# Gated linear attention followed by a Mamba output block on one core: alpha copied to SBUF ahead of its scans, idle matmuls and a new order in the first turns

## The chip, the cores and the metric

The kernel runs on one core of a Trainium2 chip. A core has engines that run side by side, each with its own stream of instructions, which it works through in the order in which the program gave them: TensorE (PE) multiplies matrices and transposes through an identity matrix, VectorE (DVE) works element by element and runs the scans, ScalarE (ACT) applies functions and copies, GpSimd (POOL) does slow element work, and SyncE (SP) only issues transfers. The engines wait for each other with semaphores. Matrix results land in PSUM, everything else lives in SBUF, inputs and outputs in device memory.

The metric is the device time of one execution in microseconds (us), as the median of several. All numbers below are of this one core.

## The reference

```python
# attention: batch 4, heads 8, sequence 768, head size 48; alpha between 0.8 and 1.0
for t in range(S):
    state = alpha[:, :, t, :, None] * state + einsum('bhd,bhde', k[:, :, t], v[:, :, t])   # outer product
    y[:, :, t] = einsum('bhd,bhde->bhe', q[:, :, t], state)
x = y.transpose(0, 2, 1, 3).reshape(4, 768, 384)          # heads side by side

# gated SSM: d_model 384, d_inner 512
proj = x @ w_in;  val, gate = proj[..., :512], proj[..., 512:]
for t in range(S):
    h = exp(A_log) * h + val[:, t];  ys[:, t] = h
out = (silu(gate) * ys) @ w_out
```

The weights and inputs of the second block come as 64-bit floats and are turned into 32-bit ones in the kernel.

## The kernel before

The sequence of each of the 4 batches is cut into 3 groups of 256 steps, which gives 12 turns, `n = 0 .. 11`. A turn has a *front* (products of the decays by scans: V from the end backwards, P from the start forwards, then K and Q scaled by them, then the scores `sc` within a block, masked into A), a *back* (block states S_n, values, result `x_sb`, and its transposition into `xT`) and the *ssm* of an earlier turn (`pj`: projection by `w_in`, scan `hh`, gate `sg`, product `f`, and `o`: projection by `w_out`). Each is a generator; a string of letters says in which order the generators are stepped, and so in which order every engine gets its instructions. F is a step of this turn's front, A of the next turn's front, B of the back, P and H of the last turn's ssm, O of the ssm two turns ago, U converts one weight unit to 32 bits (12 units), C checks the range of V, G and M start loads of later turns, L issues transfers that are waiting, E computes exp(A_log).

```python
    def front(n):
        ...
            aT = p1.tile([C, NP, GC], FP32, name="aT")
            ...
            for jj, js in enumerate(halves):                       # two halves
                tp = aT[:, js] if by_vector else turned("a", jj)   # by_vector: n >= 4. Else: TensorE transposes into PSUM
                for u in range(2):
                    nc.vector.tensor_tensor_scan(out=V[:, 2 * jj + u, GC - 1::-1], data0=tp[:, u, ::-1], ...)
                if not by_vector:
                    nc.scalar.activation(aT[:, js], tp, AF.Copy)
                yield
            K = ...                    # tp of k (TensorE), times V (VectorE)        yield
            keys_back(K, s["Kn"], ps_tp)   # tpk: TensorE; Kn: ScalarE copies       yield
            ...                        # iV0 = 1/V, P: two scans over aT, per half   yield, yield
            Q = ...                    # tp of q (TensorE), times P (VectorE)        yield
            ...                        # sc: TensorE; A: copy_predicated (VectorE)   yield

    def back(n):
        ...
            first, last = n % NG == 0, n % NG == NG - 1      # NG = 3
            S_n = p2.tile([C, GR, NP, D], FP32, name="S_n")
            if not first:
                vg = nc.vector if n < 2 else nc.gpsimd
                vg.tensor_mul(S_n[:, 0], S_end[0], s["V"][:, :, 0:1].to_broadcast([C, NP, D]))
            zv = block_states(s["Kn"], v_sb, ps_y, "y")      # z on TensorE
            ...                                              # S_n, S_end: VectorE adds   yield
            yv = values_inside(A, v_sb, ps_y, p2, 1)         # y on TensorE, then "fence" on ScalarE   yield
            values_before(yv, s["Q"], S_n, first, 1)         # y on TensorE; ScalarE copies y to x_sb  yield
            features(x_sb, xs[n], ps_tp)                     # tpx on TensorE, xT on ScalarE           yield

    def convert_unit(u):               # 2 instructions on ScalarE, 2 on VectorE, 1 on GpSimd
        ...

    def load_batch(b):                 # called by M in turns 2, 3 and 5
        t = big.tile(..., name="batch")
        ...                            # 6 memsets on GpSimd, then transfers put on the waiting list

        both = (nc.sync, nc.scalar)    # the first transfers
        load(0, "a", both, 2)
        load(0, "kq", both)
        nc.scalar.dma_start(out=a_log, ...)
        load(0, "v"); fetch_units(0, 2); load(1, "a"); fetch_units(2, 4); load(1, "k")
        fetch_units(4, 6); load(1, "q"); fetch_units(6, 8); load(1, "v")

        early = ["FFFFEFFFGBFUUAABUBCAB", "UFFUFPUFGHPBFUCUHPBAAHBPHBUU",
                 "FPHPFFUFHPUHMLFBLPLFALOLHBLABLALOLBC", "OLFFPLFFMHPLHFBLAAPLHBLACLPBHLOLB",
                 "FLFFFCLPHPLHFBMPBLAHPLBHALOBLO"]
        usual = "FLPFFFFHLPBFHWMPLBAHOLABPLHBOLC"
```

Of the kernel before, what the change touches and what calls it, by code (L numbers as in the profile page):

```python
# [18 lines left out]
def kernel(  # L19
# [185 lines left out]
    def step(gen):  # L205
        if gen is not None:
            next(gen, None)


    def ranged(ctx):  # L210
# [122 lines left out]
        def front(n):  # L333

            pad = pads[n % NBUF]
            b, g = divmod(n, NG)
            by_vector = n >= BY_VECTOR
            V = Vs[n % 2]
            s = st[n] = dict(V=V)

            def turned(name, jj):
                tp = ps_tp.tile([C, 2, GC], FP32, tag="tp", name="tp")
                for u in range(2):
                    j = 2 * jj + u
                    for c in range(G):
                        nc.tensor.transpose(tp[:, u, ds(c * C, C)], pad[name][:, c, j], ident)  # L346
                return tp

            def squares(name, dst):
                nc.vector.transpose(dst, batches[b, name][:, :, ds(g * GC, GC)])  # L350

            halves = [slice(2 * jj, 2 * jj + 2) for jj in range(NP // 2)]
            aT = p1.tile([C, NP, GC], FP32, name="aT")
            if by_vector:
                squares("a", aT)
            for jj, js in enumerate(halves):
                tp = aT[:, js] if by_vector else turned("a", jj)
                for u in range(2):
                    nc.vector.tensor_tensor_scan(out=V[:, 2 * jj + u, GC - 1::-1], data0=tp[:, u, ::-1],  # L359
                                                 data1=bias[:, 1:2].to_broadcast([C, GC]), initial=1.0,  # L360
                                                 op0=ALU.mult, op1=ALU.max)
                if not by_vector:
                    nc.scalar.activation(aT[:, js], tp, AF.Copy)
                yield
            K = p1.tile([C, NP, GC], FP32, name="K")
            if by_vector:
                squares("k", K)
            for jj, js in enumerate(halves):
                nc.vector.tensor_mul(K[:, js], K[:, js] if by_vector else turned("k", jj), V[:, js, 1:GC + 1])
            yield  # L370
            s["Kn"] = p1.tile([C, G, NP, C], FP32, name="Kn")
            keys_back(K, s["Kn"], ps_tp)
            yield
            iV0 = p2.tile([C, NP], FP32, name="iV0")
            P = p1.tile([C, NP, GC], FP32, name="P")
            for jj, js in enumerate(halves):
                nc.vector.reciprocal(iV0[:, js], V[:, js, 0])
                for u in range(2):
                    nc.vector.tensor_tensor_scan(out=P[:, 2 * jj + u, :], data0=aT[:, 2 * jj + u, :],  # L379
                                                 data1=bias[:, 1:2].to_broadcast([C, GC]),  # L380
                                                 initial=iV0[:, 2 * jj + u:2 * jj + u + 1],
                                                 op0=ALU.mult, op1=ALU.max)
                yield
            Q = s["Q"] = p2.tile([C, NP, GC], FP32, name="Q")
            if by_vector:
                squares("q", Q)
            for jj, js in enumerate(halves):
                nc.vector.tensor_mul(Q[:, js], Q[:, js] if by_vector else turned("q", jj), P[:, js])
            yield
            sc = ps_sc.tile([C, 2, 512], FP32, tag="sc", name="sc")  # L390
            scv = sc.rearrange("p i (x t) -> p i x t", t=R)
            for c in range(G):
                for j in range(NP):
                    for r in range(NR):
                        for i in range(2):
                            rows, steps = ds(DP * i, DP), ds(c * C + R * r, R)
                            nc.tensor.matmul(scv[ds(R * r, R), i, c * NP + j, :], K[rows, j, steps],
                                             Q[rows, j, steps], start=True, stop=True, skip_group_check=True)
            for i in range(2):
                nc.vector.copy_predicated(out=A[:, i].rearrange("p x t -> p (x t)"),  # L400
                                          mask=mask[:, ds(i * GP * R, GP * R)], data=sc[:, i])
            yield
# [9 lines left out]
        def back(n):  # L412

            s = st.pop(n)
            v_sb = vs.pop(n)
            first, last = n % NG == 0, n % NG == NG - 1
            S_n = p2.tile([C, GR, NP, D], FP32, name="S_n")
            if not first:
                vg = nc.vector if n < 2 else nc.gpsimd
                vg.tensor_mul(S_n[:, 0], S_end[0], s["V"][:, :, 0:1].to_broadcast([C, NP, D]))  # L420
            zv = block_states(s["Kn"], v_sb, ps_y, "y")
            S_end[0] = None if last else p2.tile([C, NP, D], FP32, name="S_end")
            for x in range(GR):
                src = zv[:, x % NR, x // NR]
                dst = S_n[:, x + 1] if x + 1 < GR else S_end[0]
                if first and x == 0:
                    nc.scalar.activation(dst, src, AF.Copy)
                elif dst is not None:
                    nc.vector.tensor_add(dst, S_n[:, x], src)  # L429
            yield  # L430
            yv = values_inside(A, v_sb, ps_y, p2, 1)
            yield
            values_before(yv, s["Q"], S_n, first, 1)
            x_sb = p1.tile([C, G, DM], FP32, name="x_sb")
            xv = x_sb.rearrange("p g (i f) -> p i g f", i=2)
            ys = yv.rearrange("p i g j e -> p i g (j e)")
            nc.scalar.activation(xv[:, 0], ys[:, 0], AF.Copy)
            for r in range(NR):
                nc.scalar.activation(xv[ds(R * r, R), 1], ys[ds(R * (1 - r), R), 1], AF.Copy)
            yield  # L440
            xs[n] = p2.tile([C, NK, GC], FP32, name="xT")
            features(x_sb, xs[n], ps_tp)
            yield
# [10 lines left out]
        for name in "aqk":  # L454
            clear_pads(1, name)
        nc.vector.memset(A, 0.0)
        both = (nc.sync, nc.scalar)
        load(0, "a", both, 2)
        load(0, "kq", both)
        nc.scalar.dma_start(out=a_log, in_=moe_A_log.rearrange("(a p) -> p a", p=C))  # L460
        load(0, "v")
        fetch_units(0, 2)
        load(1, "a")
        fetch_units(2, 4)
        load(1, "k")
        fetch_units(4, 6)
        load(1, "q")
        fetch_units(6, 8)
        load(1, "v")
        to_convert = iter(range(len(units)))  # L470

        def any_outside():
# [19 lines left out]

        early = ["FFFFEFFFGBFUUAABUBCAB", "UFFUFPUFGHPBFUCUHPBAAHBPHBUU",
                 "FPHPFFUFHPUHMLFBLPLFALOLHBLABLALOLBC", "OLFFPLFFMHPLHFBLAAPLHBLACLPBHLOLB",
                 "FLFFFCLPHPLHFBMPBLAHPLBHALOBLO"]
        usual = "FLPFFFFHLPBFHWMPLBAHOLABPLHBOLC"
        ending = ["PHRPHOPHRPHO", "OO"]
        fronts = {n: front(n) for n in range(N)}  # L500
        backs = {n: back(n) for n in range(N)}
        ssms = {}
        final = any_outside()

        def load_group(n):
            load(n + 2)
# [14 lines left out]
        with tc.manual_schedule():  # L521
            for n in range(N + 2):
                for word in early[n] if n < len(early) else usual if n < N else ending[n - N]:
# [4 lines left out]
                    elif word == "B":  # L528
                        step(backs[n])
                    elif word in "PH":  # L530
                        if n - 1 not in ssms:
                            ssms[n - 1] = ssm(n - 1, xs.pop(n - 1), prev_h, p2, ps_mm)
                        step(ssms[n - 1])
                    elif word == "O":
                        step(ssms[n - 2])
                    elif word == "C":
                        check_products(n)
                    elif word == "U":
                        convert_unit(next(to_convert))
                    elif word == "R":  # L540
                        step(final)
                    elif word == "E":
                        nc.scalar.activation(a_dec, a_log, AF.Exp)
                    elif word == "W" and n - NG - 3 in parts:
                        check_part(n - NG - 3)
                    elif word == "G":
                        load_group(n)
                    elif word == "L":
                        issue(4096 if n < NG else 3072)
                    elif word == "M":  # L550
                        make_ready(n)
# [192 lines left out]
```

## Time and profile before

| what | value |
|---|---|
| device time, median of 3 | 315.44 us (315.3 to 320.01) |
| span of the profiled execution | 312.9 us |
| ScalarE busy | 130.6 us (42%), 279 instructions |
| GpSimd busy | 44.6 us (14%), 58 instructions |
| transfers | 33.74 MB, mean 108 GB/s |
| one turn of the TensorE in its even stretch (tpk at 201.04 us to tpk at 222.87 us) | 21.83 us |
| `pj`: 576 matmul records of 128x256 | 134.6 us |
| `o`: 192 matmul records of 128x384 | 66.5 us |

How to read it: the profile lists the instructions of every engine with start and length, and for the idle time before one, which event ended it. In rows of instructions merged in order of time, the columns are start, length (both us), engine, source line, operation, result and operands, count, and in brackets the idle time before it and what ended that. A 32-bit matmul of `pj` or `o` appears as two records, a 32-bit transpose as one. PEclk is the clock that TensorE was granted, 1.00 being full.

### The profile page before, as it was taken

The numbers are of one execution on the slowest core, as the hardware profiler recorded it, in microseconds if no ns is written. First come the engines' busy times: TensorE is split into PE (matmuls) and PEld (weight loads), VectorE is DVE, ScalarE is ACT, GpSimd is POOL, SyncE is SP. The second block draws the span as 40 slices with busy tenths as digits, with TensorE's granted clock in tenths as the row PEclk, the third lists the DMA queues.
The fourth block names the chain that finished last, engine by engine and source line by source line (L and its number), as shares of the span: only waits on it lengthen the run. The fifth ranks groups of instructions, "written<-read, shape, count | busy, mean of one in ns | idle before, by whom it ended". The sixth has DMA issues, their size and how long they took to land. (4 is left out here: it accounts for less than half of the span.)

```text
span 312.9 us, 9330 instructions
## 1 busy us (share of the span) xinstructions
PE 285.9 (91%) x4041; PEld 226.3 (72%) x4041; DVE 218.3 (70%) x383; ACT 130.6 (42%) x279; POOL 44.6 (14%) x58
## 2 busy tenths in 40 slices
PE   3857997993999999999999999999999999999992
PEld 1636876881788788786787787787877877877760
DVE  4695887853728898688598796986986987932320
ACT  1338566420461561411535515625534545355120
POOL 5021410276009100055000000000000000000000
PEclk9995899997799999999999999999999999999998
DMA  8999999126769999996899998503303012000001
GB/s 134 218 259 214 177 271 166 34 40 79 108 86 172 98 116 119 118 183 111 107 112 163 125 131 145 137 2 129 78 2 127 27 57 95 5 28 26 27 31 57
DMA packets 161411, 33.74 MB, mean 108 GB/s; under 512 B 151120, under 2 KB 160336, under 8 KB 161360
## 3 DMA queue, kind: packets, MB, share of 16 engines
q1 hardware_dynamic: 157632, 32.45, 65.8%
q10 hardware_dynamic: 3728, 0.59, 1.4%
q8 instruction: 34, 0.56, 0.9%
q14 instruction: 17, 0.14, 0.2%
HBM read 28.31 MB, written 4.72 MB: 106 GB/s over the span
## 5 line engine op out<-in xcount | busy, mean ns | idle before, releaser
L121 PE MATMUL pj<-xT,w_in 128*128 128x256 f32 x576 | 134.6, 384 | 0.0
L121 PEld LDWEIGHTS pj<-xT,w_in 128*128 128x128 f32 x576 | 107.2, 191 | 16.5
L136 PE MATMUL o<-w_out,f 128*128 128x384 f32 x192 | 66.5, 491 | 0.0
L130 ACT ACTIVATE sg<-pj 128x256 f32<-128x256 f32 x48 | 18.4, 383 | 97.2 <-DVE hh L125 97.1
L136 PEld LDWEIGHTS o<-w_out,f 128*128 128x128 f32 x192 | 34.9, 190 | 20.2
L125 DVE TENSOR_TENSOR_SCAN hh<-a_dec,hh,pj 128x256 f32<-128x256 f32 x32 | 23.6, 737 | 23.0 <-PE pj L121 23.0
L131 DVE TENSOR_TENSOR f<-sg,hh 128x256 f32<-128x256 f32 x48 | 20.4, 426 | 27.4 <-ACT sg L130 27.4
L379 DVE TENSOR_TENSOR_SCAN P<-aT,iV,bias 128x256 f32<-128x256 f32 x48 | 33.9, 749 | 1.2
L257 POOL MEMSET batch<- 32x1536 f32 x18 | 24.7, 1372 | 25.1 <-DMA batch<-in_q_dram 18.4
L346 PE MATMUL tp<-ident,pads 128*128 128x128 f32 x96 | 17.4, 326 | 6.8 <-POOL mask_f L328 3.2
L420 POOL TENSOR_TENSOR S_n<-S_end,V 128x192 f32<-128x192 f32 x7 | 3.6, 514 | 140.3 <-DVE V L359 114.9
L175 PE MATMUL y<-v_sb,A 64*64 64x48 f32 x768 | 15.8, 228 | 7.6 <-DVE A L400 5.3
L175 PEld LDWEIGHTS y<-v_sb,A 64*64 64x64 f32 x768 | 13.8, 141 | 12.2 <-DVE A L400 6.9
L139 ACT ACTIVATE o_sb<-o 128x384 f32<-128x384 f32 x24 | 11.7, 488 | 22.9 <-PE o L136 20.9
L359 DVE TENSOR_TENSOR_SCAN V<-aT,bias 128x256 f32<-128x256 f32 x32 | 20.2, 677 | 0.3
L193 PEld LDWEIGHTS y<-S_n,Q 64*64 64x64 f32 x704 | 13.4, 144 | 9.2 <-ACT fence L180 4.7
L346 PEld LDWEIGHTS tp<-ident,pads 128*128 128x128 f32 x96 | 12.9, 164 | 9.6 <-POOL mask_f L328 3.2
L193 PE MATMUL y<-S_n,Q 64*64 64x48 f32 x704 | 14.9, 230 | 4.0 <-ACT fence L180 4.0
L429 DVE TENSOR_TENSOR S_n<-S_n,z 128x192 f32<-128x192 f32 x32 | 11.3, 352 | 8.6 <-POOL S_n L420 7.5
L149 ACT ACTIVATE Kn<-tpk 128x512 f32<-128x512 f32 x24 | 13.2, 594 | 9.0 <-PE tpk L148 8.2
L400 DVE COPY_PREDICATED A<-mask,sc 128x512 f32<-128x512 uint8 x24 | 16.0, 719 | 0.0
L148 PE MATMUL tpk<-ident,K 128*128 128x128 f32 x96 | 14.6, 300 | 1.5 <-ACT xT L203 1.4
(64 smaller groups left out, 303.6 us busy)
## 6 DMA issues: line engine op xcount, KB each, us to landing
v_sb<-in_v_dram SPq DMA_DIRECT2D x24, 192.0 KB, 4.7
out_dram<-o_sb SPq DMA_DIRECT2D x24, 192.0 KB, 2.6
staging<-in_moe_w_in_dram SPq DMA_DIRECT2D x8, 384.0 KB, 5.0
part<-in_moe_w_in_dram SPq DMA_DIRECT2D x8, 384.0 KB, 5.8
staging<-in_moe_w_out_dram SPq DMA_DIRECT2D x4, 384.0 KB, 6.3
batch<-in_alpha_dram SPq DMA_DIRECT2D x4, 384.0 KB, 8.0
batch<-in_k_dram SPq DMA_DIRECT2D x4, 384.0 KB, 7.5
batch<-in_q_dram SPq DMA_DIRECT2D x4, 384.0 KB, 8.5
```

Source lines behind the costliest of these rows:

```text
L121: nc.tensor.matmul(pj[:, i, :], w_in[:, kk, i, ds(cc * C, C)], xT[:, kk, :], start=(kk == 0), stop=(kk == NK - 1))
L125: nc.vector.tensor_tensor_scan(out=hh, data0=a_dec[:, cc:cc + 1].to_broadcast([C, GC]), data1=pj[:, 0, :], initial=prev_h[cc][:, GC - 1:GC ...
L130: nc.scalar.activation(sg, pj[:, 1, :], AF.Silu)
L131: nc.vector.tensor_mul(f[:, cc, :], sg, hh)
L136: nc.tensor.matmul(o, f[:, cc, ds(c * C, C)], w_out[:, cc, :], start=(cc == 0), stop=(cc == NI - 1))
L175: nc.tensor.matmul(yv[at, i, c, j, :], A[rows, i, c * NP + j, :], v_sb[rows, c, NP * i + j, :], start=(c == 0 and j == 0), stop=False, ski ...
L193: nc.tensor.matmul(yv[at, i, c, j, :], Q[rows, j, ds(R * x, R)], S_n[rows, x, j, :], start=False, stop=(c == G - 1 and j == NP - 1), skip_ ...
L257: nc.gpsimd.memset(tv[ds(DP * i + W, W), :, D - W:W], 1.0 if name == "a" else 0.0)
L346: nc.tensor.transpose(tp[:, u, ds(c * C, C)], pad[name][:, c, j], ident)
L359: nc.vector.tensor_tensor_scan(out=V[:, 2 * jj + u, GC - 1::-1], data0=tp[:, u, ::-1], data1=bias[:, 1:2].to_broadcast([C, GC]), initial=1 ...
L379: nc.vector.tensor_tensor_scan(out=P[:, 2 * jj + u, :], data0=aT[:, 2 * jj + u, :], data1=bias[:, 1:2].to_broadcast([C, GC]), initial=iV0[ ...
L400: nc.vector.copy_predicated(out=A[:, i].rearrange("p x t -> p (x t)"), mask=mask[:, ds(i * GP * R, GP * R)], data=sc[:, i])
```

## The change

The change does five things.

1. In the front, ScalarE copies the transposed alpha from PSUM into `aT` first, and the V scans read `aT`. Before, the scans read PSUM and the copy followed them.
2. In the backs of turns 1 and 2 the first product of S_n goes to VectorE; before, only that of turn 1. From turn 4 on (turn 3 has none) it stays on GpSimd.
3. A one-element-wide activation at the start makes ScalarE load its table of functions early. The k and q of turn 0 are all issued by SyncE, and weight units, k, q and v are fetched in another order.
4. A new letter D runs two matmuls of the identity with itself into an unused PSUM tile. Nothing reads it. There are 13 in turn 0 and one in turn 1.
5. The strings of turns 0 to 4 and the usual one are put in another order.

It is meant to shorten the first turns, in which the engines wait for one another, and to keep TensorE from dropping to a lower clock there.

```diff
             for jj, js in enumerate(halves):
-                tp = aT[:, js] if by_vector else turned("a", jj)
+                if not by_vector:
+                    nc.scalar.activation(aT[:, js], turned("a", jj), AF.Copy)
                 for u in range(2):
-                    nc.vector.tensor_tensor_scan(out=V[:, 2 * jj + u, GC - 1::-1], data0=tp[:, u, ::-1],
+                    nc.vector.tensor_tensor_scan(out=V[:, 2 * jj + u, GC - 1::-1], data0=aT[:, 2 * jj + u, ::-1],
                                                  ...
-                if not by_vector:
-                    nc.scalar.activation(aT[:, js], tp, AF.Copy)
                 yield
 ...
-                vg = nc.vector if n < 2 else nc.gpsimd
+                vg = nc.vector if n < NG else nc.gpsimd
 ...
-        both = (nc.sync, nc.scalar)
-        load(0, "a", both, 2)
-        load(0, "kq", both)
+        load(0, "a", (nc.sync, nc.scalar), 2)
+
+        nc.scalar.activation(bias[:, 0:1], bias[:, 0:1], AF.Copy)
         nc.scalar.dma_start(out=a_log, in_=moe_A_log.rearrange("(a p) -> p a", p=C))
-        load(0, "v")
-        fetch_units(0, 2)
-        load(1, "a")
+        load(0, "k")
+        fetch_units(0, 1)
+        load(0, "qv")
+        fetch_units(1, 2)
+        load(1, "ak")
         fetch_units(2, 4)
-        load(1, "k")
+        load(1, "q")
         fetch_units(4, 6)
-        load(1, "q")
+        load(1, "v")
         fetch_units(6, 8)
-        load(1, "v")
 ...
-        early = ["FFFFEFFFGBFUUAABUBCAB", "UFFUFPUFGHPBFUCUHPBAAHBPHBUU",
-                 "FPHPFFUFHPUHMLFBLPLFALOLHBLABLALOLBC", "OLFFPLFFMHPLHFBLAAPLHBLACLPBHLOLB",
-                 "FLFFFCLPHPLHFBMPBLAHPLBHALOBLO"]
-        usual = "FLPFFFFHLPBFHWMPLBAHOLABPLHBOLC"
+
+        early = ["DDFFDDFFUDDFFFGBUDFEDAADDCBDAUDBDB", "FFUFUFGBUFACPHBUUPHABDUPHPBHUU",
+                 "FPHPFFHUPFFHBOFMLPLCALABLHABLOLBL", "OLFFPLFAAFMLBFHPLBHPLHABLPBHLCOL",
+                 "FLFFFPLBHPLFHCPLBAHALOLBMPHBLO"]
+        usual = "FLPFFFFHLPBFHPLBHAAWMOLBPLHBOLC"
 ...
+        def warm():
+
+            t = ps_mm.tile([C, 2, GC], FP32, tag="mm", name="warm")
+            for i in range(2):
+                nc.tensor.matmul(t[:, i, 0:C], ident, ident, start=True, stop=True)
 ...
+                    elif word == "D":
+                        warm()
```

## The prediction

> **What bounds the kernel now.** I read the page first, busy shares and the 40 slices.
>
> ```profile
> PE 285.9 (91%) x4041; PEld 226.3 (72%) x4041; DVE 218.3 (70%) x383; ACT 130.6 (42%) x279; POOL 44.6 (14%) x58
> ...
> PE   3857997993999999999999999999999999999992
> ...
> POOL 5021410276009100055000000000000000000000
> PEclk9995899997799999999999999999999999999998
> ```
>
> TensorE is full from slice 12 (about 86 us) to the end: that stretch is bound by it. The holes are in the first ten slices, where the granted clock dips twice (slices 4 and 5, slices 10 and 11), each time with or after a hole. The page's chain of waits has a single link, the last copy, so I worked from the windows and from the rows in order of time. The windows (columns: stretch, length, busy us of PE, weight load, DVE, ACT, POOL with counts, granted clock, DMA share, GB/s):
>
> ```profile
> 20.00:24.00 4.00, 0.45 (x15) 0.32 (x15) 3.93 (x8) 1.05 (x2) 1.70 (x2) 0.97 0.96 260
> 24.00:28.00 4.00, 3.74 (x56) 3.35 (x56) 1.18 (x2) 2.88 (x8) 1.01 (x1) 0.50 0.95 221
> ...
> 72.00:76.00 4.00, 0.41 (x2) 0.00 (x0) 0.45 (x2) 0.00 (x0) 3.32 (x4) 0.87 0.61 77
> 76.00:84.00 8.00, 6.51 (x142) 5.52 (x143) 6.29 (x12) 2.96 (x8) 0.00 (x0) 0.64 0.76 108
> 84.00:306.00 222.00, 220.83 (x3059) 173.84 (x3058) 161.14 (x278) 93.06 (x204) 19.55 (x18) 1.00 0.64 92
> ```
>
> Two holes, each followed by half clock; after 84 us only 1.2 us of 222 are idle. Who makes the second hole, from the rows in order of time:
>
> ```profile
> 66.46 8.42 POOL L257 MEMSET batch<- 32x1536 f32 x6
> 74.96 0.51 POOL L420 TENSOR_TENSOR S_n<-S_end,V 128x192 f32<-128x192 f32 x1
> 75.51 1.13 DVE L429 TENSOR_TENSOR S_n<-S_n,z 128x192 f32<-128x192 f32 x3 [7.52 <-POOL S_n L420]
> ...
> 77.33 0.44 PE L175 MATMUL y<-v_sb,A 64*64 64x48 f32 x2 [4.92 <-DVE A L400]
> ...
> 77.93 1.95 PE L175 MATMUL y<-v_sb,A 64*64 64x48 f32 x62 [0.16 <-DVE A L400]
> ```
>
> In turn 2 the first product of S_n stands on GpSimd behind six memsets of `batch`. VectorE waits 7.52 us for it, the masked copy to A comes after it in VectorE's stream, and TensorE stands for A. The first hole:
>
> ```profile
> 7.01 1.28 ACT L363 ACT_TABLE_LOAD   x1 [7.01 <-DMA pads<-in_k_dram]
> ...
> 22.39 0.60 ACT L363 ACTIVATE aT<-tp 128x512 f32<-128x512 f32 x1 [4.20 <-DVE V L359]
> ...
> 24.26 1.95 PE L193 MATMUL y<-S_n,Q 64*64 64x48 f32 x48 [2.63 <-ACT fence L180]
> ...
> 32.54 3.49 PE L121 MATMUL pj<-xT,w_in 128*128 128x256 f32 x12
> ```
>
> ScalarE copies turn 1's alpha only after VectorE's scans, and `fence`, which the next TensorE work needs, stands behind those copies. The first projection starts at 32.54 us, at less than full clock (3.49 us; 2.7 later).
>
> **The sum of what is lost.** At full clock, start to start in the even stretch, a turn costs: tpk 0.87, four projection chunks 10.77, z 0.96, sc 1.06, y inside 1.08, y before 1.08, tpx 0.65, o 5.36, together 21.83 us, as the turn from 201.04 to 222.87 us has it; eight transposes cost 0.97 where pads are turned. I charge each stretch with its work at those prices. Up to 35.87 us: 40 transposes (4.85), two tpk (1.74), z, sc, two y (4.17), tpx (0.65), one chunk (2.69), sum 14.1, so 21.8 us are lost. To 54.60 us: work 15.9 of 18.7, 2.8 lost. From 54.60 to the o that ends near 72.3, nothing. To 82.35: work 2.65 (two y, four transposes) of 10.1, 7.4 lost. Later three small ones (102 to 105, 109 to 110, 143 to 145 us): 1.7. In all some 34 us; a change to the early order has no more to win.
>
> **What the Trainium skill says.** "TensorE: Matmul & The Clock Gate", section "What's actually happening": TensorE runs at half clock after an idle window of about 3.4 us and at full clock after about 3.4 us of work. The trace agrees: 0.45 us busy in 20 to 24, then 0.50; 4.9 us idle at 72.4, then 0.64 over 76 to 84. The same page, "Part 4: PE-mode transpose", says transposes do not count as work in the same way; no row here separates that, but it speaks for D being true matmuls. "ScalarE: Activation LUTs", section "What ACT_TABLE_LOAD costs": about 1283 ns for the load; here 1.28 us. "PSUM — Partial Sum Buffer", section "Engine vs sequencer instructions": ScalarE, VectorE and GpSimd queues are strictly first in, first out; the product at 74.96 right behind the last memset agrees.
>
> **Part by part.**
>
> *Product of turn 2 on VectorE.* One 128x192 product of 0.35 us (as turn 1's at 40.52) in place of a 7.52 us wait. VectorE was idle there, so nothing is pushed. TensorE's hole (4.9 idle plus about 2.1 of half clock in y, transposes and y, with the rest) goes: 7.4 us, of which I count 7.0 to 7.5. The next user of GpSimd's product is turn 4 (turn 3 is first in its batch); the second set of memsets can start once q of turn 3 is turned and takes 8.4 us, which ends before turn 4's back.
>
> *Alpha by ScalarE first.* Costs one 0.6 us copy before the first scan of each half, for turns 0 to 3. In turn 0: transposes of half 0 end near 5.1, copy to 5.9 (the early activation has the table in by about 5.3), scans 5.9 to 7.2, half 1 to 8.5, against 7.81 before. But K can then start on its transposes, which before waited for the table load and both copies (9.00 us): K ends near 10.8 against 11.68. In turn 1 the copies no longer wait for the scans, so `fence` is free of them.
>
> *Reordered conversions.* A unit costs VectorE 1.1 us. One now stands before P and one before the masked copy. By VectorE's stream: K to 10.8, unit to 11.9, P (3.1) to 15.1, Q (1.3) to 16.4 (15.98 before, but one unit further), S_n to 17.5, unit to 18.6, A to 20.0, V of turn 1 to 22.45. ScalarE: copies to 19.0, range check (2.7) to 21.7, fence 21.9, unit to 23.2. TensorE: y inside to 21.1, k of turn 1 to 22.4, y before to 23.7. x_sb to 25.3, xT to 26.9 (31.1 before). This is where TensorE gains, but not all of it: the built order now puts z, sc and half of turn 2's alpha ahead of the first projection. sc waits for Q of turn 1: K to 23.8, unit, P half, unit, P half, unit to 30.3, Q to 31.6. So sc 31.4 to 32.5, four transposes, and the first chunk at 33.0, no earlier than before. From there: chunk, y (A at 36.0), chunk to 39.8, transposes, y before, D, two chunks to 47.2, tpx, k of turn 2, and turn 1's first chunk at about 49.4 against 54.60. Gain 5.2 us.
>
> *Idle matmuls.* 14 D of two 128x128 matmuls; half of a 256-wide one (2.69/6 = 0.45), so 0.45 us each at full clock, 6.3 in all. They lie almost all in gaps (turn 0 has more than 20 us of them); in the walk above they are included. What they buy is that I may use full-clock prices: before, transposes and tpk from 9.0 to 13.1, and everything from 24 to 34, ran at about double length.
>
> *Order in turns 2 to 4 and after.* I followed the built order with the durations above through turn 2: every wait of TensorE (K at 51.8, Q at 60.1, A near 65) ends before its turn in the stream. The third turn's tpk comes near 76.3 against 89.29, 13.0 earlier, which is the sum of the two gains (12.6) and small change. TensorE's order in the usual turn is unchanged.
>
> Sum: 5.2 + 7.4 = 12.6. I take off about 0.5 for new small waits that a walk by hand does not see: 315.4 - 12.1 = 303.3, rounded to 303.
>
> **The rivals.**
>
> *Transfers become the limit.* The first 20 loads run at about 200 GB/s without a pause until 44 us, in both kernels. v of turn 1 is now the 14th load of about 0.39 MB, 5.5 MB, which by the bytes moved before (4.9 MB at 24 us, 5.8 at 28) lands near 27.5, when z wants it; alpha of turn 2 lands near 32.7, wanted at 32.5. So there is no margin, and SyncE issues four more transfers. If this binds, the prologue gains 2 instead of 5: 306. For: those figures. Against: no long wait on a transfer now.
>
> *The clock drops all the same.* By the walk TensorE stands from 29.6 to 31.3 and in several gaps before. If half clock returns about 29 to 36 us, 2 to 3 us come back: 305 to 306.
>
> *The hole moves.* If VectorE, now the bound of the first 36 us, or PSUM buffers stop TensorE in turns 2 to 4, part of the 7.4 returns: 305 to 308. For: three scan blocks in a row before Q of turn 3. Against: VectorE had 11.5 us of work in 54 to 72 and slack of some 5 us per turn.
>
> *Better than the walk.* The 1.7 us of late holes close and the prologue gains 7: 300.
>
> **Range and chances.** 303.0, and 299.5 to 308 for 8 in 10; upward is wider since three of four rivals point there. The turn 2 product alone is worth 2.3%, so the first parts would have to lose for the whole to stay within 2% (309.1): faster 0.93, same 0.05, slower 0.02.
>
> **What would show it.** In the profile after: the wait of S_n on GpSimd at 7.5 us gone and TensorE without a hole between turn 2's o and y; xT of turn 0 near 27; the first chunk still near 33; turn 1's first chunk near 49; tpk of turn 3 near 76; PEclk without the two dips; turns of 21.8 us from there. I am wrong if z waits for v, if half clock shows about 30, or if a turn after the third is longer than 21.9.

## The result and the profile after

The changed kernel takes 305.9 us (median of four executions, 304.69 to 307.32) against 315.64 us (four, 315.3 to 320.01): a ratio of 0.9662, with a 95% interval from 0.9567 to 0.9758. The prediction was 303.0 us, in a range of 299.5 to 308. So the direction and most of the size came out, and about 3 us of the expected gain are missing. The ratios here and below are not quotients of the medians, and they leave out disturbed executions, which medians and ranges hold, so the two can differ a little.

The 40 slices of the page of the changed kernel (TensorE, GpSimd, granted clock):

```profile
PE   7988699999999999999999999999999999999991
...
POOL 5111321283092000190000000000000000000000
PEclk9999999999999999999999999999999999999998
```

The hole in slice 10 is gone, and so are both dips of the clock. What remains is the 6 in slice 5 (30.3 to 37.8 us). Its stretches in the windows (columns as before: length, busy us of PE, weight load, DVE, ACT, POOL, granted clock, DMA share, GB/s):

```profile
24.00:28.00 4.00, 3.07 (x44) 2.38 (x36) 3.90 (x7) 2.56 (x6) 1.01 (x1) 1.00 1.10 269
28.00:32.00 4.00, 2.61 (x74) 1.95 (x72) 3.93 (x8) 3.90 (x8) 1.45 (x2) 1.00 1.04 268
32.00:36.00 4.00, 2.56 (x71) 2.11 (x72) 3.76 (x10) 0.32 (x1) 0.87 (x2) 1.00 0.76 127
72.00:76.00 4.00, 4.00 (x76) 2.67 (x75) 3.52 (x8) 1.73 (x4) 0.00 (x0) 1.00 0.59 74
```

From 72 to 76 us TensorE works all the time (0.41 us of 4 before). From 24 to 36 it has full clock, but is busy for 8.24 of 12 us only. The rows of TensorE there say what it waits for:

```profile
30.99 0.68 PE L160 MATMUL z<-v_sb,Kn 64*64 64x48 f32 x32 [0.81 <-DMA v_sb<-in_v_dram]
32.08 1.53 PE L396 MATMUL sc<-Q,K 64*64 64x64 f32 x64 [0.41 <-DVE Q L387]
34.34 0.30 PE L346 MATMUL tp<-ident,pads 128*128 128x128 f32 x1 [0.73 <-DMA pads<-in_alpha_dram]
35.13 0.52 PE L346 MATMUL tp<-ident,pads 128*128 128x128 f32 x3 [0.49 <-DMA pads<-in_alpha_dram]
35.48 2.76 PE L121 MATMUL pj<-xT,w_in 128*128 128x256 f32 x12
```

Three waits are new: half of z stands for v of turn 1, sc for Q, and the transposes for turn 2's alpha, in two pieces. They hold back the first projection chunk to 35.48 us (33.0 in the walk), although its operand `xT` is ready at 27.4. The third turn in order of time, GpSimd, VectorE and TensorE mixed:

```profile
62.25 8.45 POOL L257 MEMSET batch<- 32x1536 f32 x6
...
66.07 0.35 DVE L419 TENSOR_TENSOR S_n<-S_end,V 128x192 f32<-128x192 f32 x1
66.53 1.13 DVE L428 TENSOR_TENSOR S_n<-S_n,z 128x192 f32<-128x192 f32 x3
...
70.09 1.15 PE L175 MATMUL y<-v_sb,A 64*64 64x48 f32 x64
```

The product is done on VectorE in 0.35 us while the memsets run, and the 64 records of y follow without a wait.

Where the time went, by marks on TensorE in the two profiled executions (spans 312.9 and 302.7 us):

| mark | before | after | gained up to here | predicted |
|---|---|---|---|---|
| first chunk of turn 0 starts | 32.54 | 35.48 | -2.9 | -0.5 |
| first chunk of turn 1 starts | 54.60 | 51.87 | 2.7 | 5.2 |
| tpk of turn 3 starts | 89.29 | 79.19 | 10.1 | 13.0 |
| from there to the end (length) | 223.6 | 223.5 | 10.2 | 12.1 (12.6 less 0.5) |

So 7.4 us came between the second and third mark, and 2.7 of 5.2 before the second. After the third, nothing changes: a turn is still 21.83 us, tpk to tpk (124.78 to 146.61). The profiled execution is the fastest of the four; the median lost about 1 us more.

### The profile page after: what moved, and what is told of

Its sections match the earlier page's. It is cut to its first block, busy times and chain, and to the rows that moved or that the text cites. A ratio compares the mean times of both kernels' runs of the same rounds, so it can differ in the third digit from the quotient of the medians.

```text
span 302.7 us, 9427 instructions
## 1 busy us (share of the span) xinstructions
PE 288.3 (95%) x4097; PEld 229.7 (76%) x4097; DVE 221.0 (73%) x384; ACT 131.5 (43%) x280; POOL 44.4 (15%) x57
## 5 line engine op out<-in xcount | busy, mean ns | idle before, releaser
L378 DVE TENSOR_TENSOR_SCAN P<-aT,iV,bias 128x256 f32<-128x256 f32 x48 | 35.8, 788 | 0.8
L360 DVE TENSOR_TENSOR_SCAN V<-aT,bias 128x256 f32<-128x256 f32 x48 | 29.6, 673 | 5.7 <-ACT aT L358 5.4
L257 POOL MEMSET batch<- 32x1536 f32 x18 | 24.7, 1371 | 23.9 <-PE tp L346 13.1
L346 PE MATMUL tp<-ident,pads 128*128 128x128 f32 x96 | 15.8, 302 | 2.1 <-DMA pads<-in_alpha_dram 1.2
L396 PE MATMUL sc<-Q,K 64*64 64x64 f32 x768 | 14.4, 221 | 1.9 <-DVE Q L387 1.4
L193 PEld LDWEIGHTS y<-S_n,Q 64*64 64x64 f32 x704 | 12.2, 134 | 5.1 <-issue 5.0
L125 DVE TENSOR_TENSOR_SCAN hh<-a_dec,pj 128x256 f32<-128x256 f32 x16 | 10.9, 679 | 7.1 <-PE pj L121 7.1
L346 PEld LDWEIGHTS tp<-ident,pads 128*128 128x128 f32 x96 | 12.0, 153 | 4.8 <-DMA pads<-in_alpha_dram 2.0
L160 PEld LDWEIGHTS z<-v_sb,Kn 64*64 64x64 f32 x768 | 12.4, 134 | 4.3 <-issue 3.3
L175 PEld LDWEIGHTS y<-v_sb,A 64*64 64x64 f32 x768 | 12.5, 134 | 4.0 <-issue 1.9
L396 PEld LDWEIGHTS sc<-Q,K 64*64 64x64 f32 x768 | 12.6, 135 | 3.7 <-DVE Q L387 2.8
```

The costliest lines, as they stand in the source:

```text
L125: nc.vector.tensor_tensor_scan(out=hh, data0=a_dec[:, cc:cc + 1].to_broadcast([C, GC]), data1=pj[:, 0, :], initial=prev_h[cc][:, GC - 1:GC ...
L257: nc.gpsimd.memset(tv[ds(DP * i + W, W), :, D - W:W], 1.0 if name == "a" else 0.0)
```

## The experiments

Three theories were to be told apart. **Alpha late**: the missing time is turn 2's alpha, which lands after the walk's 32.7 us. **VectorE late**: Q of turn 1 is late since VectorE's work takes longer beside GpSimd's additions. **Clock**: half clock in some executions. And each part of the change was to be valued by itself. Kernels of a group share their chip and their executions of the kernel before: 315.31 us in the first group, 315.71 in the second and 315.93 in the third.

### First group: the parts

**The changed kernel again**, with no edit:

> The changed kernel once more, as the yardstick on this chip and for a second trace. Both theories: 304.5 to 307.5 us, ratio to before about 0.968. If the spread of its earlier executions (304.7 to 307.3) comes from TensorE's clock, a slower execution shows a stretch of half clock in the first 40 us that the first trace (mean clock 0.997) does not have.

Measured: 306.36 us (306.1 to 309.03), ratio 0.9733 [0.967, 0.9796]. TensorE's rows in its profiled execution (span 304.2 us):

```profile
35.80 0.87 PE L346 MATMUL tp<-ident,pads 128*128 128x128 f32 x3 [0.86 <-DMA pads<-in_alpha_dram]
36.46 4.00 PE L121 MATMUL pj<-xT,w_in 128*128 128x256 f32 x12
```

Alpha's last piece is 0.7 us later than in the first profile, and the same 12 records of the first chunk take 4.00 instead of 2.76 us; the granted clock is 0.63 from 36 to 40 us. The third turn's tpk starts at 80.83 (79.19). So the rival of the prediction in which the clock drops all the same came true here, after the wait for alpha. The first chunk is 1.2 us longer by it; 0.7 of that is left at turn 1's first chunk, which starts at 53.50.

**The turn 2 product alone**, in the kernel before:

```diff
-                vg = nc.vector if n < 2 else nc.gpsimd
+                vg = nc.vector if n < NG else nc.gpsimd
```

> The kernel before with one line changed: the first product of S_n of turn 2 on VectorE. Theory 1 (the product behind the memsets alone makes the hole of turn 2): 7 to 7.5 us less, about 308, ratio 0.977, TensorE without a hole between turn 2's o and y. Theory 2 (the hole moves, the new order of turns 2 to 4 is needed as well): 2 to 5 us less, and another wait stands before y of turn 2.

Measured: 309.0 us (307.64 to 310.33), 0.9794 [0.9734, 0.9855]. The hole is gone (y follows o directly at 71.62 us), and tpk of turn 3 starts at 81.72, 7.6 us earlier than in the kernel before. 0.7 of that is already there at turn 1's first chunk (53.88 against 54.60), which comes ahead of the edit, so the hole gave 6.9. Of the 7.6, 1.08 us return at 86.44, where transposes wait for ScalarE's copy of Kn of turn 3, and 6.4 us are left of the span. That is a little less than the first theory said. The rest of the change adds some 2.6 us by the medians (309.0 to 306.36); the intervals of the two ratios overlap.

**Without the idle matmuls** (all the rest of the change):

```diff
                     elif word == "D":
-                        warm()
+                        pass
```

> The changed kernel without the 14 pairs of idle matmuls (D does nothing); all else the same. Theory 1 (VectorE's chain and the transfers set the first 36 us, the idle matmuls only keep the clock up): half clock returns somewhere between 12 and 30 us, and 1 to 3 us are lost. Rival (the clock carries most of what the first turns gain): 4 to 6 us slower than the changed kernel. Second rival (they only stand in the way): 0.5 to 1 us faster, because k of turn 0 is transposed earlier.

Measured: 308.24 us (306.51 to 312.2), 0.975 [0.9675, 0.9826], which overlaps with the kernel that has them. Without them the clock is 0.76 from 24 to 28 us and 0.81 from 28 to 32, yet TensorE reaches turn 0's y before at 21.96 instead of 23.33 us and ends sc of turn 1 at 31.7 instead of 33.6. All of that lead is lost in one row:

```profile
34.73 0.30 PE L346 MATMUL tp<-ident,pads 128*128 128x128 f32 x1 [2.98 <-DMA pads<-in_alpha_dram]
```

Alpha comes when it comes, whether TensorE waits 3 us for it or 0.8. After a second wait of 0.59 us the clock is 0.57 from 36 to 40 us, and the first chunk takes 4.44 us. So a lead of TensorE is lost as long as alpha is late; the median is 1.9 us above that of the kernel with the idle matmuls, which fits the first theory, but the overlap leaves it open.

**The turn 2 product back on GpSimd**, in the changed kernel:

```diff
-                vg = nc.vector if n < NG else nc.gpsimd
+                vg = nc.vector if n < 2 else nc.gpsimd
```

> The changed kernel with the product of turn 2 back on GpSimd. The memsets run from 62.25 to 70.7 us in the changed kernel, and y of turn 2 starts at 70.09. Theory 1: the product comes at about 70.8, S_n and A follow to 73.3, y moves to about 72.5 to 73.5, so 2.5 to 4 us slower than the changed kernel, with or without half clock after it. Rival (the product is worth 7.4 us in any order): 7 to 8 us slower.

Measured: 306.48 us (305.61 to 308.18), 0.9699 [0.965, 0.9748]: no slower. Both theories missed. The third turn, mixed engines:

```profile
64.31 0.90 POOL L419 TENSOR_TENSOR S_n<-S_end,V 128x192 f32<-128x192 f32 x1
...
65.27 8.45 POOL L257 MEMSET batch<- 32x1536 f32 x6
...
72.26 1.15 PE L175 MATMUL y<-v_sb,A 64*64 64x48 f32 x64
```

In the new string of turn 2 (`FPHPFFHUPFFHBOFML...`) B stands ahead of M; in the old one (`FPHPFFUFHPUHMLFB...`) M came first. GpSimd so gets the product ahead of its six memsets. From turn 1's first chunk (54.03) to turn 3's tpk (81.36) TensorE takes 27.33 us here, 27.32 in the changed kernel and 34.69 before. So the hole has two cures, either of which is enough: another engine for the product in the old order, or the rest of the change with the old engine. That it is the place of B and M in it is read from these rows; the two letters were not moved by themselves.

### Second group: why the first turns gained less

**The changed kernel**, as the yardstick:

> The changed kernel as the yardstick beside the next three: 305 to 307 us. In the first trace the first projection of turn 0 started at 35.48 us at full clock, in the second at 36.46 at about half clock, both after a wait for alpha of turn 2. Theory: every execution has that wait, and the half clock comes with the longer ones.

Measured: 307.16 us (305.8 to 309.77), 0.9743 [0.9703, 0.9784]. In its profile TensorE waits 1.29 and 0.72 us for the two pieces of alpha, and the first chunk runs from 36.38 at full clock (2.75 us). These waits are the longest of the three profiles of this kernel, so half clock does not go with the longer ones, as the theory had it. Its third turn's tpk is at 80.10.

**Turn 2's alpha fetched ahead of weight units 6 and 7**; nothing else is moved but these two units, which come after it:

```diff
         load(1, "v")
-        fetch_units(6, 8)
 ...
-            load(n + 2)
             if n == 0:
+                load(2, "a")
+                fetch_units(6, 8)
+                load(2, "kqv")
                 fetch_units(8, ...)
+            else:
+                load(n + 2)
```

> The changed kernel with alpha of turn 2 fetched ahead of weight units 6 and 7 instead of behind them; nothing else differs. Theory (the transfer of alpha of turn 2 is what the first projection waits for): alpha lands near 31 to 32, the waits at 34 to 36 us go, the first projection starts near 34.0, at full clock, 1.5 to 3 us faster than the changed kernel. Rival (VectorE's chain up to Q of turn 1 is the bound all the same): the projection starts earlier but VectorE's scans and products behind it do not, and turn 1's first chunk stays at 51.9 or later; 0 to 0.5 us.

Measured: 303.66 us (302.49 to 304.29), 0.9621 [0.9592, 0.9649]: 3.5 us less than the yardstick, and with no overlap of the executions. SyncE's issues for that alpha in the changed kernel:

```profile
28.43 3.23 SPq L110 DMA_DIRECT2D pads<-in_alpha_dram  x4
```

and in this one:

```profile
25.93 4.37 SPq L110 DMA_DIRECT2D pads<-in_alpha_dram  x4
```

and TensorE here:

```profile
31.49 1.53 PE L396 MATMUL sc<-Q,K 64*64 64x64 f32 x64
32.95 0.97 PE L346 MATMUL tp<-ident,pads 128*128 128x128 f32 x4
33.76 2.75 PE L121 MATMUL pj<-xT,w_in 128*128 128x256 f32 x12
```

The issues start 2.5 us earlier, no wait for alpha is left, the four transposes are in one piece behind sc, and the first chunk starts at 33.76, near the walk's 33.0. Turn 1's first chunk is at 50.16 (49.4 in the walk). **Alpha late** is confirmed as a cause. How much of the 3.5 us it carries is less clear: at turn 3's tpk, two profiles with alpha early (77.48 here, 79.02 in the repeat below) are on average 1.8 us ahead of three of the changed kernel (79.19, 80.83, 80.10). The rest of the difference of the medians was not traced.

**Without GpSimd's additions in the weight conversion.** A unit is converted from 64 to 32 bits by two bit operations on VectorE, and GpSimd adds in the low bits. Here that addition is left out, so the weights keep their upper bits only; the time is of a kernel with 12 instructions less on GpSimd.

```diff
-            nc.gpsimd.tensor_add(units[u][0].bitcast(I32), units[u][0].bitcast(I32), lo.bitcast(I32))
```

> The changed kernel without GpSimd's addition of the low bits of the converted weights; the weights keep only their upper bits. Theory (VectorE's scans of two operands in SBUF and its SBUF-only bit operations run long while GpSimd adds): P in turn 0 takes 1.40 us per half instead of 2.11, P in turn 1 1.40 instead of 2.22, the bit operation at 30.25 us 0.56 instead of 1.17; Q of turn 1 is done some 2 us earlier. The first projection still waits for alpha of turn 2, so the time falls by less than 1 us. Rival (the long scans have another cause): they stay long.

Measured: 307.9 us (304.18 to 310.03), 0.9672 [0.963, 0.9713]. The profiled execution took 310.0 us, so I take only lengths of single instructions from it. VectorE beside GpSimd in the changed kernel:

```profile
25.01 2.22 DVE L378 TENSOR_TENSOR_SCAN P<-aT,iV,bias 128x256 f32<-128x256 f32 x2
25.03 1.01 POOL L298 TENSOR_TENSOR w_in<-w_in,staging 128x384 int32<-128x384 int32 x1 [4.91 <-ACT x_sb L436]
...
30.00 1.01 POOL L298 TENSOR_TENSOR w_in<-w_in,staging 128x384 int32<-128x384 int32 x1 [3.96 <-ACT staging L293]
30.25 1.17 DVE L296 SCALAR_TENSOR_TENSOR w_in<-staging,w_in 128x384 uint32<-128x384 uint32 x1
```

and the same pair of scans without the addition:

```profile
24.78 1.40 DVE L377 TENSOR_TENSOR_SCAN P<-aT,iV,bias 128x256 f32<-128x256 f32 x2
```

A pair of scans takes 1.40 us alone and 2.22 beside an addition, the bit operation 0.56 and 1.17. So the mechanism of **VectorE late** is real: three such meetings in the first two turns, about 2 us. What it is worth while alpha is late stays open. The ratio rests on the executions of 304.18, 305.38 and 306.45 us alone; their middle one is 1.8 us below the yardstick (307.16), and the intervals of the two ratios just touch. With alpha early, the next run, it is worth nothing that can be seen.

**Both edits:**

> Both: alpha of turn 2 ahead of units 6 and 7, and GpSimd's addition left out. Theory (two bounds one behind the other, transfers first, then VectorE): more than the sum of the two alone, the first projection near 32 to 33 us, 3 to 4.5 us faster than the changed kernel. Rival (v of turn 1 is the next to bind, landing near 30.5 to 31): the first projection not before 33.5, no more than e6 alone brings plus 0.5.

Measured: 303.46 us (302.2 to 306.06), 0.9622 [0.958, 0.9665], the same as with alpha alone, so the rival holds and not the theory. VectorE now starts Q of turn 1 at 29.85 us (31.35), and the next wait takes its place:

```profile
30.89 1.48 PE L160 MATMUL z<-v_sb,Kn 64*64 64x48 f32 x64 [1.37 <-DMA v_sb<-in_v_dram]
```

z waits for v of turn 1, which the prediction had named as a landing without margin (27.5).

### Third group: what is left

**Alpha early again**, the same kernel as above:

> The kernel with alpha of turn 2 ahead of units 6 and 7 once more, as the yardstick beside the next three: 302.5 to 304.5 us, ratio to before about 0.962, the first projection at 33.5 to 34.5 us at full clock.

Measured: 303.83 us (302.4 to 304.8), 0.9614 [0.9573, 0.9655], as before. In its profiled execution no wait for alpha is left, but sc waits 0.86 us for Q, the clock is 0.60 from 32 to 36 us, and the first chunk starts at 35.27 and takes 3.23 us; turn 1's first chunk comes at 51.70. So the expected start, at full clock, was met in one of two profiles, and half clock is not excluded by alpha early.

**Alpha early, without idle matmuls:**

> The same without the idle matmuls. With alpha late they hid nothing that could be seen (308.2 against 306.4 us, within the spread). Theory: half clock at 24 to 30 us as in the run with late alpha, perhaps again to 36, TensorE otherwise 1 to 1.5 us earlier in turn 0; together 0.5 to 2.5 us slower than the yardstick. Rival (the idle matmuls now only stand in the way): 0.5 to 1.5 us faster.

Measured: 302.59 us (301.96 to 303.24), 0.9585 [0.9547, 0.9623]: the lowest median of all kernels. Against the kernel with idle matmuls it is 1.2 us, with overlapping intervals, so the rival is likelier than the theory but not shown. TensorE's rows:

```profile
30.73 1.36 PE L396 MATMUL sc<-Q,K 64*64 64x64 f32 x64
...
32.67 2.76 PE L121 MATMUL pj<-xT,w_in 128*128 128x256 f32 x12
```

The clock is 0.62 from 24 to 28 us here, and still sc starts 0.8 and 1.5 us earlier than in the two profiles with the idle matmuls (31.49 and 32.27), and turn 1's first chunk is at 48.65 (50.16 and 51.70). The clock is full again from 28.5 us on, and from 24.7 to then TensorE had run only transposes (tpx, tpk, tp; z starts at 29.14). In the kernel before, transposes from 26.14 to 29.80 did not bring it back (0.50 up to 32 us). So the prediction's question whether transposes count as work stays open.

**Alpha early, with turn 1's loads and the weight units in turn:**

```diff
-        load(1, "ak")
-        fetch_units(2, 4)
+        load(1, "a")
+        fetch_units(2, 3)
+        load(1, "k")
+        fetch_units(3, 4)
         load(1, "q")
-        fetch_units(4, 6)
+        fetch_units(4, 5)
         load(1, "v")
-        fetch_units(6, 8)
+        fetch_units(5, 6)
 ...
+                load(2, "a")
+                fetch_units(6, 8)
+                load(2, "kqv")
```

> The same with the weight units spread between the loads of turn 1: alpha, unit 2, k, unit 3, q, unit 4, v, unit 5. Theory (in 16 to 20 us the changed kernel moves 130 to 175 GB/s against 266 before, because eight small transfers in a row leave too few bytes under way): the rate in 16 to 20 us rises above 200 GB/s, v of turn 1 lands before 30 us, and 0.3 to 1 us are gained over the yardstick. Rival (the rate has another cause): it stays below 180 and k of turn 1 comes later, 0 to 2 us slower.

Measured: 303.82 us (303.36 to 304.72), 0.9621 [0.9582, 0.966]: no gain. The rate from 16 to 20 us rose from 158 to 187 GB/s, less than the theory asked for, and from 20 to 24 it fell from 232 to 180. z no longer waits for v, but sc then waits 1.43 us for Q. Why transfers move less from 16 to 20 us than before the change (175 GB/s against 266) stays open.

**Product on VectorE, copy ahead of the scans, and the early activation, in the old order.** The k and q of turn 0 are issued by SyncE and ScalarE as before, and the activation stands between ScalarE's issues for alpha and those for k and q.

```diff
             for jj, js in enumerate(halves):
-                tp = aT[:, js] if by_vector else turned("a", jj)
+                if not by_vector:
+                    nc.scalar.activation(aT[:, js], turned("a", jj), AF.Copy)
                 ...                                     # the scans read aT
-                vg = nc.vector if n < 2 else nc.gpsimd
+                vg = nc.vector if n < NG else nc.gpsimd
 ...
         load(0, "a", both, 2)
+        nc.scalar.activation(bias[:, 0:1], bias[:, 0:1], AF.Copy)
         load(0, "kq", both)
```

> The kernel before with three parts only: the product of turn 2 on VectorE, ScalarE's copy of alpha ahead of the scans, and the early activation; old order, old loads, no idle matmuls. Theory (the copies no longer make fence wait for the scans): fence of turn 0 comes near 21 to 22 us instead of 24.0, the first projection near 30 to 31 instead of 31.8 (the product alone), 1 to 2.5 us faster than the product alone (ratio 0.979). Rival (VectorE's chain in turn 0 only gets longer by the copy, 0.6 us): no difference to the product alone, or 0.5 us slower.

Measured: 309.35 us (307.36 to 310.84), 0.9793 [0.9744, 0.9842], equal to the product alone (0.9794). ScalarE and VectorE at the start:

```profile
6.50 0.38 ACTq L460 DMA_DIRECT2D a_log<-in_moe_A_log_dram  x1
6.91 1.28 ACT L458 ACT_TABLE_LOAD   x1 [6.91 <-DMA pads<-in_k_dram]
...
9.00 2.44 DVE L360 TENSOR_TENSOR_SCAN V<-aT,bias 128x256 f32<-128x256 f32 x4 [6.99 <-ACT aT L358]
```

The table comes at 6.91 us, when ScalarE is through with its issues (a_log is the last), although in the program the activation stands ahead of those for k and q; why, no run shows. In the changed kernel, which took k and q away from ScalarE, it comes at 3.52, again right behind a_log (3.12). The scans, which need the copy now, so start at 9.00 us. `fence` of turn 0 is free of turn 1's copies as meant, but y itself, which it waits for, is late, and `fence` comes at 23.43 instead of the expected 21 to 22. The profile is 1.1 us ahead of the product alone at turn 3's tpk (80.59 against 81.72) and loses it behind that (226.1 against 224.8 us to the end), which was not traced. So the copy and the activation in this place are worth nothing that can be seen; what they are worth with the loads and the order of the changed kernel was not tried apart.

## Why the prediction came out as it did

**The product of turn 2** was right in size: 7.4 us predicted, 7.4 between the marks, 6.9 with the product alone. Two points of the step did not hold. In the changed kernel the line is not needed, as I followed the new strings for TensorE and VectorE and did not note that they also put GpSimd's product ahead of the memsets; with the product back on GpSimd the stretch is as short (27.33 us). The number would have come out without the line too, and that is luck. And "nothing is pushed" was too kind: in the old order, 1.08 us came back one turn later.

**The first turns** gave 2.7 us in place of 5.2, and this is the term that was mis-sized. The walk took 32.7 us for turn 2's alpha, from bytes moved by the kernel before. Its last piece came some 2.4 us later (the three transposes at 35.13, behind a wait). The rival "Transfers become the limit" put the time for this at 306, and 305.9 was measured. The edit that fetches alpha earlier took 3.5 us off the median, and in one of its two profiles the walk's first chunk (33.0) and turn 1's first chunk (49.4) are nearly met, 33.76 and 50.16.

The mistake was to read a landing from bytes moved. From 16 to 20 us the changed kernel moves less (175 GB/s against 266), but up to 32 us both move 205 on average, so the rate is not it. SyncE issues that load in the kernel before at

```profile
27.06 4.35 SPq L110 DMA_DIRECT2D pads<-in_alpha_dram  x4
```

The last of the four pieces is issued at 30.9 us there and lands 3.1 us later, at 34.0; in the changed kernel it is issued at 30.8 and lands 4.2 us later, at 35.0. So 1.3 of the 2.4 us stood in the trace of the kernel before, in which TensorE did not have to wait for this load, and about 1 us came with the change. The walk was also off for v of turn 1: its own figures (5.5 MB; 4.9 at 24 us, 5.8 at 28) give 26.6 and not 27.5, and TensorE waits for the second half of it until 30.99.

**Alpha by ScalarE first and the new conversions**: xT of turn 0 was to end at 26.9 and ends at 27.4, against more than 30 before. That is right, and of no use while alpha is late, as the walk had said for sc in its place. VectorE's stream, where I took 3.1 us for P, was too fast: Q of turn 1 ended at 32.6 instead of 31.6, since scans and bit operations take longer beside GpSimd. The Trainium skill has this in "GPSIMD Engine Reference", section "1. Specifications" (GpSimd shares its SBUF interfaces with VectorE, with contention for instructions with two SBUF inputs); it gives no size, and the run without the additions shows it: 1.40 to 2.22 us.

**The idle matmuls**: "They lie almost all in gaps" is not so: y before of turn 0 starts at 23.33 us with them and at 21.96 without. "What they buy" cannot be told from nothing: the clock stays full from 24 to 32 us with them, but without them the median is 1.9 us higher while alpha is late and 1.2 us lower with alpha early, and both differences lie within overlapping intervals.

**The clock**: the page had no dip, so that the rival looked wrong; the second execution shows it, after alpha. TensorE was idle there in pieces of 0.69, 0.82 and 0.86 us, none near the 3.4 us that the prediction reckoned with, and half clock followed. It followed too with the product back on GpSimd, whose first turns are in the same order (pieces of 0.22, 1.29 and 0.75 us, first chunk 4.03 us); in the yardstick pieces of 0.49, 1.29 and 0.72 us left the clock full. The Trainium skill, "TensorE: Matmul & The Clock Gate", section "What's actually happening", says that a free-running window is watched and that the same kernel differs from run to run, and these profiles do differ; whether the window is the cause here no run shows. The mean granted clock of an execution goes with its time: of the 14 executions of the changed kernel, the four with a clock below 0.986 took 307.32 to 309.77 us, the other ten 304.69 to 307.25. This does not tell whether half clock makes an execution long or comes with longer waits. The rest of a span, after turn 3's tpk, differs by 3 us between the executions profiled (223.1 to 226.1), which was not traced either.

**The hole moves** came true only in small: turns 2 to 4 are full in the first profile, and in the two others sc of turn 3 waits 0.46 and 0.74 us for Q, which the rival had named. **Better than the walk** did not come true, though alpha early without idle matmuls (302.59) comes to within 0.4 us of the predicted time. Of the three signs that I said would prove me wrong, z waiting for v came true in all profiles of the changed kernel (0.58 to 0.81 us), half clock in one of three, and at about 36 instead of 30 us; the even turn stayed at 21.83.

## What to carry to other kernels

When an order of loads changes, take the landing times load by load, from when each is issued and how long such a load took to land in the trace at hand, and not from bytes over time; where the walk shows a landing with no margin, count that rival as the main line. When a slow instruction stands in front of a short one on an engine with a queue, look first at the order in which the two are issued: a new order cured here what another engine cured too. Matmuls that are only to keep the clock up have to be tried without, as they stand in the same queue as the work.

## What the runs showed of the hardware

VectorE's instructions with their operands in SBUF become longer beside a GpSimd addition of 1.0 us: in the changed kernel two 128x256 scans 2.11 to 2.23 instead of 1.40 us, a 128x384 bit operation 1.07 to 1.26 instead of 0.56. Q, which reads PSUM, keeps its length (1.28 us with an addition beside it, 1.26 without). It is not always VectorE that loses: in the run without idle matmuls an addition that begins at 13.91 us, when the second of two scans (13.18 to 14.57) has just begun, takes 1.46 us, and the scans keep 1.39.

Idle matmuls from 1.6 us on brought TensorE to its pace only at about 11 us. Rows of TensorE in the changed kernel:

```profile
6.28 1.92 PE L510 MATMUL warm<-ident 128*128 128x128 f32 x8
7.99 2.23 PE L346 MATMUL tp<-ident,pads 128*128 128x128 f32 x8
...
11.71 1.06 PE L510 MATMUL warm<-ident 128*128 128x128 f32 x8
```

Eight records take 1.92 us at 6.28 and 1.06 at 11.71, while the clock record shows full all along. Without the idle matmuls eight transposes still take 1.51 us at 11.96; with them, those at 12.61 take 1.04. So in the first 11 us the record cannot be read as the pace of TensorE; the length of a known instruction can.
